# The second transform stage of a fused filter and gated network as three products of high and low parts

## The chip, the core and the metric

The kernel runs on one core of a Trainium2 chip. The metric is the device time of one execution in microseconds (us). Five engines work side by side and meet at semaphores: PE (matrix products), ACT (ScalarE), DVE (VectorE), POOL (GpSimd) and SP (SyncE, which here only issues transfers). Each engine takes its own instructions in the order in which the program lists them. SBUF is the memory on the core, PSUM the banks into which PE writes its sums, DRAM the large memory outside.

## The reference, cut to what matters

```python
X = np.fft.rfft(x, axis=1)                     # x: 8 batches x 3136 x 256
x = np.fft.irfft(X * (filt_r + 1j * filt_i), n=3136, axis=1)
h = np.maximum(x @ w_in, 0.0)                  # 256 -> 1024
conv = sum(conv_w[k] * shifted(h, k - 1) for k in range(3))
out = (h * sigmoid(conv)) @ w_out              # 1024 -> 256
```

Eight batches pass through a filter in the frequency domain, and then through a network whose gate is a convolution of three taps along the sequence.

## The kernel before, in words

**The transform.** A batch has 3136 = 112 x 28 rows of 256 numbers. The transform and its way back are four stages of matrix products, each with 14 operations (`NP`), one for every pair `q` of the 28. The first stage, kind "1", multiplies two blocks of x by tables (`by_column`, L243 to L245, four products in the trace for two in the program). Its sums go from PSUM to SBUF by an ACT copy (`store`, L238 to L241) and from there to DRAM (`a_dram`). The second stage, kind "2", reads them back in another order of rows (`load_in`, L233) and multiplies all 512 columns by one table (`second`, L254, through `by_row`, L247 to L252). `filt` (L260 to L268) multiplies these sums by the filter with three DVE instructions that read the PSUM bank, and POOL adds two parts to `z`. The third stage, kind "3", multiplies `z` by another table (L249 too, operand `z`), and its sums go through `store` to `b_dram`. The fourth, kind "4", reads them back (L275) and leaves the network's input `y`. All four stages are products of fp32 operands.

**The network.** `inner` (L187 to L189) makes one bank of 512 columns of h for one of 8 blocks of 128 features: six products of fp32r operands, that is `mm3` (high by high, high by low, low by high) for two blocks of 128 inputs. `project` makes 12 fp32r products of 256 columns (L536 to L538).

**The order.** The first batch's transform runs alone, in front of the main loop, and ends with two operations "1" of the second batch (`AHEAD`, L402 to L405). The main loop has one iteration, here called a slot, for each block of 510 rows and 128 features, 400 in all, and everything in it stands in program order (`manual_schedule`). A list, `plan`, names for each slot the transform operations of the next batch: 48 slots belong to each batch. Slots are numbered from 0 within the 48 of a batch; batch 1 is the first whose transform lies in the loop, batch 7 the last. For slot m the program lists, in this order:

1. `from_bank` for the transform operations of slot m-1: the ACT copy for kinds "1" and "3", the three DVE instructions for kind "2", a DVE copy for kind "4";
2. `want_in`, which asks for loads ahead;
3. on PE the transform operations of slot m, and then `inner` of slot m;
4. on ACT `relu` and the middle tap `centre` of the network's slot m-1 (L495, L500), then `sigmoid` of slot m-2 (L507); on DVE the first tap of slot m-1 (L504); on ACT the rounding of slot m-3 (L156);
5. on DVE the `gate` of slot m-2 (L510); on POOL the low part of g for slot m-4 (L162); then the steps in a list `later`;
6. on DVE the third tap of slot m-1 (L504), and on PE `project` of slot m-6.

The transform operations share two PSUM banks (pool `ps_t`, `bufs=2`), which they take in turn as they are free. An operation that takes a bank waits until the last reader of the operation that held it before is through. Because PE goes by its list, the `inner` behind such an operation waits too.

Of the kernel before, what the change touches and what calls it, by code (L numbers as in the profile page):

```python
# [132 lines left out]
def tile_fft_filter_gated_ffn(  # L133
# [58 lines left out]
    a_dram = [dram.tile([N2, 112, D], F32, name=f"a_dram{b}") for b in range(B)]  # L192
    b_dram = [dram.tile([N2, 112, D], F32, name=f"b_dram{b}") for b in range(B)]
    a_out = [t[:].rearrange("n p d -> p n d") for t in a_dram]
    a_in = [t[:].rearrange("n (r g) d -> (n r) g d", g=G) for t in a_dram]
# [6 lines left out]
    s2_sb = wc.tile([112, 120], F32, name="s2_sb")  # L202
    s2s_sb = wc.tile([112, 120], F32, name="s2s_sb")
    s3_sb = wc.tile([120, 112], F32, name="s3_sb")
    s3s_sb = wc.tile([120, 112], F32, name="s3s_sb")
    one_sb = wc.tile([128, 128], F32, name="one_sb")
# [26 lines left out]
    def load_in(pool, kind, b, q, bufs, tag):  # L233
        r = pool.tile([112, 2, D], F32, name=tag, bufs=bufs)
        nc.sync.dma_start(out=r, in_={"1": xv, "2": a_in, "4": b_in}[kind][b][:, pair(q)])
        return r

    def store(pool, kind, b, q, ps, bufs, tag, queue=nc.sync):  # L238
        st = pool.tile([112, 2, D], F32, name=tag, bufs=bufs)
        nc.scalar.activation(st, ps[0:112].rearrange("p (j d) -> p j d", d=D), AF.Copy)  # L240
        queue.dma_start(out={"1": a_out, "3": b_out}[kind][b][:, pair(q)], in_=st)  # L241
# [12 lines left out]
    def second(ps, q, r):  # L254
        by_row(ps[0:120], q, r, s2_sb, s2s_sb)

# [28 lines left out]
    def load_weights(k, pool):  # L285
        raws[k] = raw = pool.tile([128, 2, 1024], I32, name="raw", bufs=1 if pool is tp else 2)
        for part, w in enumerate((w_in, w_out)):
            nc.sync.dma_start(out=raw[:, part], in_=w[:, 1024 * k:1024 * k + 1024])
# [7 lines left out]
    def convert(k, pool, n=2):  # L296

        for j in range(2):
            em = pool.tile([128, 2, 2, 256], I32, name="em", bufs=n)
            w = pool.tile([128, 2, 256], F32, name="ws", bufs=n)  # L300
            yield from to_f32(w, raws[k][:, :, 512 * j:512 * j + 512], em[:, 0], em[:, 1])
# [10 lines left out]
    with (  # L312
# [4 lines left out]
        fts, tabs, rows, zs, pss = {}, {}, {}, {}, {}  # L317
        by_r = [sc.tile([120, 4, N2], F32, name=f"by_r{i}", bufs=1) for i in range(2)]
# [32 lines left out]
        with tc.tile_pool(name="sq", bufs=2) as sq:  # L351
# [15 lines left out]
            def first_loads(c):  # L367
                table("1", c)
                r = sq.tile([128, 4, D], F32, name="rows", bufs=5)
# [12 lines left out]
            for q in range(NP):  # L382
                if q % 2 == 0 and q // 2 + 3 < 7:
                    first_loads(q // 2 + 3)
                if q == 8:
                    for k in range(4):
                        load_filter(k)
                    load_weights(2, sc)
                ps = turned_stage(rows["x", q // 2][:, 2 * (q % 2):2 * (q % 2) + 2], [tab("1", q)[:, j] for j in range(2)])
                nc.scalar.activation(at[:, :, pair(q)], ps, AF.Copy)  # L390
                if q >= 1:
                    steps(early, 3 if q < 12 else 2 * (q == 12))
            for t, s in zip(by_r, (s3_sb, s3s_sb)):
                nc.gpsimd.tensor_copy(t, s.rearrange("p (c r) -> p r c", r=4))
            for i in range(NP + 4):
# [18 lines left out]
                if i == 5:  # L414
                    table("1", 0)
                    for q in range(AHEAD):
                        r = sq.tile([128, 2, D], F32, name="xa", bufs=2)
# [189 lines left out]
    stored = {("1", 1): AHEAD}  # L607
# [5 lines left out]
    def want_in():  # L613
        while wanted["in"] < min(done["in"] + 5, len(inputs)) and ready(inputs[wanted["in"]]):
            op = inputs[wanted["in"]]
            wanted["in"] += 1
            got_in[op] = load_in(tp, *op, 5, "tin")
# [13 lines left out]
    def transform(op):  # L631
# [20 lines left out]
    def from_bank(op):  # L652
# [12 lines left out]
    def to_y(op):  # L665
        kind, b, q = op
        if kind == "4":
# [6 lines left out]
    with tc.manual_schedule(engines=COMPUTE | {mybir.EngineType.SP}):  # L674
# [4 lines left out]
        late = convert(3, wp, 1)  # L679
# [80 lines left out]
```

## Time and profile before

| what | before |
|---|---|
| median of 3 runs | 1554.33 us (1551.63 to 1555.62) |
| profiled execution | 1554.59 us |
| its span, first to last instruction | 1552.8 us |
| DVE busy | 1185.3 us, 76% |
| ACT busy | 1144.7 us, 74% |
| POOL busy | 828.3 us, 53% |
| mean clock of PE as granted | 0.997 |
| moved by DMA | 229.49 MB, mean 148 GB/s |

The profile is one execution with the start and length of each instruction. Its duration is not that by which a stream of products advances: products overlap in PE's pipeline, so the step from one start to the next is what a product costs there. A bracket at the end of a timeline row says how long the engine had been idle before the instruction and what released it. The profiled execution's own time is 1.8 us above its span.

### The profile page before, as it was taken

To read this page: it belongs to the slowest core of one execution; us is meant where nothing else is said; L and a number is where in the kernel's file an instruction comes from. 1 tells how busy PE (TensorE), PEld (TensorE's weight loads), DVE (VectorE), ACT (ScalarE), POOL (GpSimd) and SP (SyncE) were. 2 spreads that over 40 slices of the span, in tenths; PEclk is the share of its full clock that TensorE was granted. 3 is DMA by queue.
4 is the path that set the end of the run, shared out by engine and by line. 5 is a ranking of instruction groups with operands and counts; after the bars stand their busy time and mean duration, and the time that the engine had idled before them with its cause. 6 is when DMAs were issued, how large, how long until landed. Compare 5 with 4: busy or idle time off the path is not lost.

```text
span 1552.8 us, 26446 instructions
## 1 busy us (share of the span) xinstructions
PE 1519.7 (98%) x9202; PEld 1290.6 (83%) x9202; DVE 1185.3 (76%) x1810; ACT 1144.7 (74%) x1973; POOL 828.3 (53%) x721
## 2 busy tenths in 40 slices
PE   6999999999999999999999999999999999999999
PEld 5777788877997789877898778987799878999998
DVE  7978766788677877778777776778867888777776
ACT  3576668766896668866787667976688667888886
POOL 4644447545574555645565445744557445664444
PEclk9999999999999999999999999999999999999999
DMA  8867653665436555465544665356543543300000
GB/s 302 256 185 215 208 170 109 181 200 166 135 110 202 179 155 159 121 193 169 177 124 143 185 196 153 97 179 203 165 135 100 160 140 110 101 28 15 28 28 30
DMA packets 158436, 229.49 MB, mean 148 GB/s; under 512 B 16432, under 2 KB 109088, under 8 KB 158304
## 3 DMA queue, kind: packets, MB, share of 16 engines
q1 hardware_dynamic: 157824, 227.35, 48.4%
q8 instruction: 73, 1.20, 0.3%
q14 instruction: 59, 0.48, 0.1%
q10 hardware_dynamic: 480, 0.46, 0.1%
HBM read 157.10 MB, written 70.65 MB: 147 GB/s over the span
## 4 chain that ended last, share of the span: by engine, by line
PE 92%; DVE 2%; ACT 2%; DMA 2%; issue 2%; SPq 0%; POOL 0%; ACTq 0%; POOLq 0%; DVEq 0%
PE ps_h L187 12%; PE ps_h L189 12%; PE ps_h L188 12%; PE po L536 12%; PE po L538 12%; PE po L537 11%; PE ps_t L249 10%; PE ps_t L275 6%; PE ps_t L245 5%; DMA rows<-in_x 1%; PE ps_t L252 1%; ACT br L346 0%; DVE v L265 0%; DVE z L264 0%; DMA f<-in_filt 0%
## 5 line engine op out<-in xcount | busy, mean ns | idle before, releaser
L504 DVE SCALAR_TENSOR_TENSOR t<-ps_h,cw,t 128x510 f32<-128x510 f32 (+1 forms) x800 | 589.1, 737 | 301.5 <-ACT t L500 298.4
L162 POOL TENSOR_TENSOR g<-t,g 128x510 fp32r<-128x510 f32 (+1 forms) x400 | 505.3, 1273 | 203.6 <-ACT g L156 191.9
L536 PE MATMUL po<-wo,g 128*128 128x256 f32 (+1 forms) x1576 | 440.4, 279 | 0.1
L538 PE MATMUL po<-wo,g 128*128 128x256 f32 (+1 forms) x1576 | 439.5, 279 | 0.0
L537 PE MATMUL po<-wo,g 128*128 128x256 f32 (+1 forms) x1576 | 439.3, 279 | 0.0
L495 ACT ACTIVATE ps_h<-ps_h 128x512 f32<-128x512 f32 (+1 forms) x400 | 234.7, 587 | 243.9 <-PE ps_h L189 242.2
L500 ACT ACTIVATE t<-ps_h,cw 128x510 f32<-128x510 f32 (+1 forms) x400 | 272.4, 681 | 102.8 <-POOL g L162 70.1
L267 POOL TENSOR_TENSOR z<-z,v 120x512 f32<-120x512 f32 x112 | 144.8, 1293 | 380.4 <-DVE v L266 312.7
L187 PE MATMUL ps_h<-y,wi 128*128 128x512 f32 (+1 forms) x688 | 333.4, 485 | 0.5 <-DVE y L159 0.5
L536 PEld LDWEIGHTS po<-wo,g 128*128 128x128 f32 (+1 forms) x1576 | 297.0, 188 | 17.3 <-ACT g L156 0.3
L537 PEld LDWEIGHTS po<-wo,g 128*128 128x128 f32 (+1 forms) x1576 | 296.4, 188 | 17.0
L538 PEld LDWEIGHTS po<-wo,g 128*128 128x128 f32 (+1 forms) x1576 | 296.6, 188 | 0.6 <-POOL g L162 0.5
L189 PE MATMUL ps_h<-y,wi 128*128 128x512 f32 (+1 forms) x688 | 270.1, 393 | 0.0
L188 PE MATMUL ps_h<-y,wi 128*128 128x512 f32 (+1 forms) x688 | 270.1, 393 | 0.0
L510 DVE TENSOR_TENSOR t<-ps_h,t 128x510 f32<-128x510 f32 (+1 forms) x400 | 268.6, 671 | 0.9 <-ACT t L507 0.8
L507 ACT ACTIVATE t<-t 128x510 f32<-128x510 f32 (+1 forms) x400 | 245.3, 613 | 1.7 <-DVE t L504 1.6
L156 ACT ACTIVATE g<-t 128x510 fp32r<-128x510 f32 (+1 forms) x400 | 245.1, 613 | 0.2 <-DVE t L510 0.2
L162 POOL TENSOR_TENSOR y<-z,y 128x448 fp32r<-128x448 f32 x98 | 138.5, 1422 | 93.8 <-ACT y L156 91.9
L187 PEld LDWEIGHTS ps_h<-y,wi 128*128 128x128 f32 x688 | 130.4, 189 | 44.3 <-issue 23.6
L188 PEld LDWEIGHTS ps_h<-y,wi 128*128 128x128 f32 x688 | 130.7, 190 | 41.3 <-issue 24.3
L189 PEld LDWEIGHTS ps_h<-y,wi 128*128 128x128 f32 x688 | 130.0, 189 | 30.2 <-POOL wi L162 0.3
L240 ACT ACTIVATE st<-ps_t 112x512 f32<-112x512 f32 x194 | 114.0, 590 | 11.2 <-PE ps_t L245 11.1
(91 smaller groups left out, 1608.0 us busy)
## 6 DMA issues: line engine op xcount, KB each, us to landing
filt<-in_filt SPq DMA_DIRECT2D x98, 512.0 KB
tin<-a_dram SPq DMA_DIRECT2D x98, 224.0 KB
b_dram<-st SPq DMA_DIRECT2D x98, 224.0 KB
tin<-b_dram SPq DMA_DIRECT2D x98, 224.0 KB
tin<-in_x SPq DMA_DIRECT2D x96, 224.0 KB
a_dram<-st SPq DMA_DIRECT2D x96, 224.0 KB
out<-ot SPq DMA_DIRECT2D x45, 256.0 KB
tab<-in_m SPq DMA_DIRECT2D x98, 98.0 KB
```

The source lines that it names most:

```text
L156: nc.scalar.activation(dst, src, AF.Copy)
L162: nc.gpsimd.tensor_tensor(out=dst, in0=src, in1=hi.bitcast(F32), op=ALU.subtract)
L187: nc.tensor.matmul(ps, lhsT=wh, rhs=rh, start=start, stop=False, **kw)
L188: nc.tensor.matmul(ps, lhsT=wh, rhs=rl, start=False, stop=False, **kw)
L189: nc.tensor.matmul(ps, lhsT=wl, rhs=rh, start=False, stop=stop, **kw)
L500: nc.scalar.activation(t, hs[u, f][:, 1:n + 1], AF.Copy, scale=cw[:, 1, f:f + 1])
L504: nc.vector.scalar_tensor_tensor(out=t, in0=h[:, k:place(u)[2] + k], scalar=cw[:, k, f:f + 1], in1=t, op0=ALU.mult, op1=ALU.add)
L507: nc.scalar.activation(ts[u, f], ts[u, f], AF.Sigmoid)
L510: nc.vector.tensor_mul(ts[u, f], hs.pop((u, f))[:, 1:place(u)[2] + 1], ts[u, f])
L536: nc.tensor.matmul(o, lhsT=gh[:, c:c + n], rhs=wo[0][:, f], start=first, stop=False, skip_group_check=True)
L537: nc.tensor.matmul(o, lhsT=gh[:, c:c + n], rhs=wo[1][:, f], start=False, stop=False, skip_group_check=True)
L538: nc.tensor.matmul(o, lhsT=gl[:, c:c + n], rhs=wo[0][:, f], start=False, stop=last, skip_group_check=True)
```

## The change

The second stage of the seven batches in the loop becomes `mm3`: three fp32r products of 512 columns in place of one fp32 product. Its table is cut once, by four POOL instructions at the end of the first batch's first stage, into a high part and what is left. The sums of the first stage are cut as they leave their bank: ACT writes the high part where the copy stood, and a new DVE instruction subtracts it from the sum, read from the bank once more, and writes the low part. Both go to DRAM (`a_dram`, and the new `r_dram`), and both are loaded, 224 KB each, for the second stage. The DVE instruction and its transfer stand in `later`, behind the gate and ahead of the third tap; only then is the operation counted as stored. To make room, loads for kind "2" get a pool of their own (`tia`, 3 buffers), `tin` has 3 buffers in place of 5, the tiles for stores become two of `st` and two of `sh`, `rows` has 4 in place of 5, and the early conversion of weights borrows `tia` and `st`. The first batch's second stage stays one fp32 product.

```diff
-        st = pool.tile([112, 2, D], F32, name=tag, bufs=bufs)
...
+    def split_store(pool, b, q, ps, queue=nc.sync):
+        st = pool.tile([112, 2, 2, D], F32R, name="sh", bufs=2)
+        p = ps[0:112].rearrange("p (j d) -> p j d", d=D)
+        hi_act(st[:, 0], p)
+        queue.dma_start(out=a_out[b][:, pair(q)], in_=st[:, 0].bitcast(F32))
+
+        def rest():
+            lo_dve(st[:, 1], p, st[:, 0])
+            queue.dma_start(out=r_out[b][:, pair(q)], in_=st[:, 1].bitcast(F32))
+        return rest
...
+    def load_in(pool, kind, b, q):
+        if kind == "2":
+            r = pool.tile([112, 2, 2, D], F32R, name="tia", bufs=3)
+            for h, t in enumerate((a_in, r_in)):
+                nc.sync.dma_start(out=r[:, h].bitcast(F32), in_=t[b][:, pair(q)])
+            return r
+        r = pool.tile([128, 2, D], F32, name="tin", bufs=3)[0:112]
...
+    def second_split(ps, q, r):
+        if q < NP - 1:
+            mm3(ps[0:120], *second_parts[0], *(r[:, h].rearrange("p j d -> p (j d)") for h in range(2)))
+        else:
+            for j, parts in enumerate(second_parts):
+                mm3(ps[0:120, j * D:j * D + D], *parts, r[:, 0, j], r[:, 1, j])
...
+            for (h, l), t in zip(second_parts, (s2_sb, s2s_sb)):
+                nc.gpsimd.tensor_copy(h, t)
+                lo_pool(l, t, h)
...
-                    store(tp, "1", 1, i - NP, ps, 3, "st", nc.scalar)
+                    split_store(tp, 1, i - NP, ps, nc.scalar)()
...
-        while wanted["in"] < min(done["in"] + 5, len(inputs)) and ready(inputs[wanted["in"]]):
+        while wanted["in"] < min(done["in"] + 6, len(inputs)) and ready(inputs[wanted["in"]]):
             op = inputs[wanted["in"]]
+            if sum((o[0] == "2") == (op[0] == "2") for o in got_in) == 3:
+                break
...
-            second(ps, q, r)
+            second_split(ps, q, r)
...
-        if kind in "13":
-            store(tp, kind, b, q, ps, 3, "st")
+        if kind == "1":
+            rests[op] = split_store(tp, b, q, ps)
+        if kind == "3":
+            store_third(tp, b, q, ps)
...
+        if kind == "1":
+            def rest():
+                rests.pop(op)()
+                stored[kind, b] = stored.get((kind, b), 0) + 1
+            return rest
```

Line numbers in the rows below are those of the kernel before where the row is of before, and of the changed kernel otherwise: there L187 to L189 are the three products of `mm3`, L261 is `by_column`, L265 a product of the third stage, L256 the store of the third stage, L156 a high part on ACT, L159 a low part on DVE, L544 a tap, L550 the gate, L288 to L290 the filter, L535, L540 and L547 `relu`, `centre` and `sigmoid`.

On PE, batch 3, slot 23, before: an operation of the third stage and one of the second, each with what it waits for. The two wait for a bank through ACT's and DVE's semaphore:

```order
L249 MATMUL ps_t_5847<-z_5749,s3_sb_78 112x512 [waits Activation_49,Pool_49]
L249 MATMUL ps_t_5849<-tin_5610,s2_sb_76 120x512 [waits DMAHW7_49,DVE_49]
```

The same place of the changed kernel:

```order
L265 MATMUL ps_t_6089<-z_5986,s3_sb_88 112x512 [waits DVE_49,Pool_49]
L187 MATMUL ps_t_6091<-tia_5916,s20_84 120x512 [waits DMAHW4_49,Activation_49]
L188 MATMUL ps_t_6091<-tia_5916,s20_84 120x512 [waits DMAHW5_49]
L189 MATMUL ps_t_6091<-tia_5916,s21_85 120x512
```

The two banks have changed places. The operation of the second stage takes the bank of the third-stage operation just ahead of it, and so waits for the ACT instruction that stores `ps_t_6089`. That instruction, the last of these rows of ACT, stands behind the network's work of one slot:

```order
L156 ACTIVATE sh_6084<-ps_t_6049 112x512 [waits DMAHW6_49,DMAHW0_49,PE_49]
L535 ACTIVATE ps_h_6054<-ps_h_6054 128x512 [waits PE_49]
L540 ACTIVATE t_6105<-ps_h_6054,cw_90 128x510 [waits Activation_49,Pool_49]
L547 ACTIVATE t_6062<-t_6062 128x510 [waits DVE_49]
L156 ACTIVATE g00_924<-t_6014 128x510 [waits PE_49]
L256 ACTIVATE st_6127<-ps_t_6089 112x512 [waits DMAHW6_49,PE_49]
```

On DVE, the start of batch 1 in the changed kernel, slot 2: `sh_1017` and `sh_1020` are the tiles for slot 1's two operations of the first stage, `t_1045` belongs to the network's slot 1, `t_1006` to its slot 0:

```order
L544 SCALAR_TENSOR_TENSOR t_1045<-ps_h_998,cw_90,t_1045 128x510 [waits Activation_49]
L550 TENSOR_TENSOR t_1006<-ps_h_966,t_1006 128x510 [waits Activation_49]
L159 TENSOR_TENSOR sh_1017<-ps_t_988,sh_1017 112x512 [waits DMAHW3_49,DMAHW1_49,PE_49]
L159 TENSOR_TENSOR sh_1020<-ps_t_993,sh_1020 112x512 [waits DMAHW4_49,DMAHW2_49,PE_49]
L544 SCALAR_TENSOR_TENSOR t_1045<-ps_h_998,cw_90,t_1045 128x510 [waits DVE_49]
```

The two L159 are new; the banks `ps_t_988` and `ps_t_993` are read by them last, where ACT's copy was the last reader before.

More of the change, by code (lines that the diff above doesn't have):

```diff
@@ L192, in tile_fft_filter_gated_ffn @@
     a_dram = [dram.tile([N2, 112, D], F32, name=f"a_dram{b}") for b in range(B)]
+    r_dram = [dram.tile([N2, 112, D], F32, name=f"r_dram{b}") for b in range(B)]
     b_dram = [dram.tile([N2, 112, D], F32, name=f"b_dram{b}") for b in range(B)]
-    a_out = [t[:].rearrange("n p d -> p n d") for t in a_dram]
-    a_in = [t[:].rearrange("n (r g) d -> (n r) g d", g=G) for t in a_dram]
+    a_out, r_out = ([t[:].rearrange("n p d -> p n d") for t in ts] for ts in (a_dram, r_dram))
+    a_in, r_in = ([t[:].rearrange("n (r g) d -> (n r) g d", g=G) for t in ts] for ts in (a_dram, r_dram))
     b_out = [t[:].rearrange("n (r g) d -> (n r) g d", g=G) for t in b_dram]
@@ L201, in tile_fft_filter_gated_ffn @@
     wc = ctx.enter_context(tc.tile_pool(name="wc", bufs=1))
-    s2_sb = wc.tile([112, 120], F32, name="s2_sb")
-    s2s_sb = wc.tile([112, 120], F32, name="s2s_sb")
+    second_parts = [[wc.tile([112, 120], F32R, name=f"{n}{h}") for h in range(2)] for n in ("s2", "s2s")]
     s3_sb = wc.tile([120, 112], F32, name="s3_sb")
     s3s_sb = wc.tile([120, 112], F32, name="s3s_sb")
-    one_sb = wc.tile([128, 128], F32, name="one_sb")
     cw = wc.tile([128, 3, NF], F32, name="cw")
@@ L231, in pair, with store_third @@
         return slice(2 * q, 2 * q + 2)
-    def load_in(pool, kind, b, q, bufs, tag):
-        r = pool.tile([112, 2, D], F32, name=tag, bufs=bufs)
-        nc.sync.dma_start(out=r, in_={"1": xv, "2": a_in, "4": b_in}[kind][b][:, pair(q)])
-        return r
-    def store(pool, kind, b, q, ps, bufs, tag, queue=nc.sync):
-        st = pool.tile([112, 2, D], F32, name=tag, bufs=bufs)
+    def load_in(pool, kind, b, q):
[5 more added lines that the diff above has]
+        r = pool.tile([128, 2, D], F32, name="tin", bufs=3)[0:112]
+        nc.sync.dma_start(out=r, in_={"1": xv, "4": b_in}[kind][b][:, pair(q)])
+        return r
+    def split_store(pool, b, q, ps, queue=nc.sync):
[7 more added lines that the diff above has]
+        return rest
+    def store_third(pool, b, q, ps):
+        st = pool.tile([128, 2, D], F32, name="st", bufs=2)[0:112]
         nc.scalar.activation(st, ps[0:112].rearrange("p (j d) -> p j d", d=D), AF.Copy)
-        queue.dma_start(out={"1": a_out, "3": b_out}[kind][b][:, pair(q)], in_=st)
+        nc.sync.dma_start(out=b_out[b][:, pair(q)], in_=st)
     def by_column(ps, w, r):
@@ L285, in load_weights @@
     def load_weights(k, pool):
-        raws[k] = raw = pool.tile([128, 2, 1024], I32, name="raw", bufs=1 if pool is tp else 2)
+        if pool is tp:
+            raws[k] = [pool.tile([128, 2, 2, D], F32R, name="tia", bufs=3).rearrange("p a j d -> p a (j d)").bitcast(I32) for _ in range(2)]
+            for j in range(2):
+                for part, w in enumerate((w_in, w_out)):
+                    nc.sync.dma_start(out=raws[k][j][:, part], in_=w[:, 1024 * k + 512 * j:1024 * k + 512 * j + 512])
+            return
+        raws[k] = raw = pool.tile([128, 2, 1024], I32, name="raw", bufs=2)
         for part, w in enumerate((w_in, w_out)):
@@ L294, in convert_conv, with convert @@
         yield from to_f32(cw.rearrange("p (o k) f -> p o (k f)", o=1), conv_raw, e, m)
-    def convert(k, pool, n=2):
+    def convert(k, pool):
         for j in range(2):
-            em = pool.tile([128, 2, 2, 256], I32, name="em", bufs=n)
-            w = pool.tile([128, 2, 256], F32, name="ws", bufs=n)
-            yield from to_f32(w, raws[k][:, :, 512 * j:512 * j + 512], em[:, 0], em[:, 1])
+            if pool is tp:
+                if j == 0:
+                    em = pool.tile([128, 2, 2, D], F32R, name="tia", bufs=3).bitcast(I32)
+                w, raw = pool.tile([128, 2, D], F32, name="st", bufs=2), raws[k][j]
+            else:
+                em = pool.tile([128, 2, 2, 256], I32, name="em", bufs=2)
+                w, raw = pool.tile([128, 2, 256], F32, name="ws", bufs=2), raws[k][:, :, 512 * j:512 * j + 512]
+            yield from to_f32(w, raw, em[:, 0], em[:, 1])
             halves = [(t[0][:, j, 256 * k:256 * k + 256], t[1][:, 2 * k + j]) for t in zip(wi, wo)]
@@ L317, in tile_fft_filter_gated_ffn @@
         fts, tabs, rows, zs, pss = {}, {}, {}, {}, {}
+        s2_sb, s2s_sb = (sc.tile([112, 120], F32, name=n, bufs=1) for n in ("s2_sb", "s2s_sb"))
+        one_sb = sc.tile([128, 128], F32, name="one_sb", bufs=1)
         by_r = [sc.tile([120, 4, N2], F32, name=f"by_r{i}", bufs=1) for i in range(2)]
@@ L368, in first_loads @@
                 table("1", c)
-                r = sq.tile([128, 4, D], F32, name="rows", bufs=5)
+                r = sq.tile([128, 4, D], F32, name="rows", bufs=4)
                 nc.sync.dma_start(out=r, in_=xt[0:128, 4 * c:4 * c + 4])
@@ L416, in tile_fft_filter_gated_ffn @@
                     for q in range(AHEAD):
-                        r = sq.tile([128, 2, D], F32, name="xa", bufs=2)
+                        r = tp.tile([128, 2, D], F32, name="tin", bufs=3)
                         nc.sync.dma_start(out=r, in_=xt[N1:N1 + 128, pair(q)])
@@ L605, in tile_fft_filter_gated_ffn @@
     got_in, got_table, got_filter, got_z, banks, vs = {}, {}, {}, {}, {}, {}
-    stored = {("1", 1): AHEAD}
+    stored, rests = {("1", 1): AHEAD}, {}
     def ready(op):
@@ L613, in want_in @@
     def want_in():
-        while wanted["in"] < min(done["in"] + 5, len(inputs)) and ready(inputs[wanted["in"]]):
+        while wanted["in"] < min(done["in"] + 6, len(inputs)) and ready(inputs[wanted["in"]]):
             op = inputs[wanted["in"]]
+            if sum((o[0] == "2") == (op[0] == "2") for o in got_in) == 3:
+                break
             wanted["in"] += 1
-            got_in[op] = load_in(tp, *op, 5, "tin")
+            got_in[op] = load_in(tp, *op)
     def want_table(n):
@@ L678, in tile_fft_filter_gated_ffn @@
         want_filter(0)
-        late = convert(3, wp, 1)
+        late = convert(3, tp)
         for m in range(NF * NU + PLAG + 1):
```

## The prediction

> **What bounds the kernel now.** I read the page first, then the busy time of a long stretch of the loop, then the timeline of single slots.
>
> ```profile
> span 1552.8 us, 26446 instructions
> PE 1519.7 (98%) x9202; PEld 1290.6 (83%) x9202; DVE 1185.3 (76%) x1810; ACT 1144.7 (74%) x1973; POOL 828.3 (53%) x721
> PE 92%; DVE 2%; ACT 2%; DMA 2%; issue 2%; SPq 0%; POOL 0%; ACTq 0%; POOLq 0%; DVEq 0%
> 500.00:700.00 200.00, 199.01 (x1177) 166.97 (x1176) 151.16 (x231) 148.69 (x254) 107.00 (x90) 1.00 0.55 163
> ```
>
> PE is busy for 98% of the span and holds 92% of the chain that ended last. In the window (stretch, length, busy PE, PE's weight loads, DVE, ACT, POOL, clock, share of DMA, GB/s) PE lacks 1 us in 200, at full clock. So time that PE saves is time saved, and any wait put ahead of PE is lost at full price: DVE's and ACT's 25% of idle time doesn't help if one of their instructions comes late.
>
> **The products.** Next come rows of PE's timeline (start, duration, engine, line); what a product costs is the step between starts.
>
> ```profile
> 502.75 0.40 PE L189 MATMUL ps_h<-y,wi 128*128 128x512 f32 x1
> 503.44 0.39 PE L189 MATMUL ps_h<-y,wi 128*128 128x512 f32 x1
> 505.06 1.02 PE L249 MATMUL ps_t<-z,s_sb 120*112 120x512 f32 x2
> 505.92 1.03 PE L245 MATMUL ps_t<-tin,tab 112*112 112x256 f32 x4
> ```
>
> Three fp32r products of 512 columns, from one L189 to the next, step by 0.69 us, 0.23 each. One fp32 product of 512 columns (two records) steps by 0.86. The new second stage therefore saves 0.86 - 0.69 = 0.17 to 0.18 us in each of 98 operations: **-17.4 us**, 2.5 in each of seven batches. The two last pairs in halves (L252) are taken at the same price.
>
> The Trainium skill, "FP8 and Floating Point Precision", section "TensorE Precision Notes", counts four passes for true FP32. By that rule three products save a quarter of 0.86, as an estimate 0.215 us an operation and 21 us in all; the rows above show 3.8 passes, and the sum keeps them.
>
> **What the parts cost.** ACT's high part stands where the copy stood and has its shape. The low part is new on DVE; no such subtraction from PSUM is in the trace, and its nearest row is L264, with as many columns from PSUM and a second operand.
>
> ```profile
> L240 ACT ACTIVATE st<-ps_t 112x512 f32<-112x512 f32 x194 | 114.0, 590 | 11.2 <-PE ps_t L245 11.1
> L264 DVE TENSOR_TENSOR z<-ps_t,filt 120x512 f32<-120x512 f32 x98 | 66.9, 683 | 1.3 <-DMA filt<-in_filt 1.1
> ```
>
> So a low part is 0.69 us (bounds 0.6, the step of a gate from below, and 0.75, a tap). As work on DVE, 98 x 0.69 = 68 us, it fits into 370 us of idle time, and by itself costs nothing. What counts is that a bank of the first stage is now released by DVE, behind the tap and the gate of the slot, and that which operation gets which of the two banks has shifted. From the counts on which the built program's PE waits, I took the releaser of each bank, before and after. Four kinds of wait are new or longer.
>
> **(a) A bank released by the store of the same slot.** The rows to read are one slot's: the last product of an `inner` and the next transform operation on PE, ACT's four instructions, and DVE's tap.
>
> ```profile
> 499.78 0.40 PE L189 MATMUL ps_h<-y,wi 128*128 128x512 f32 x1
> 501.43 1.02 PE L249 MATMUL ps_t<-tin,s_sb 112*120 112x512 f32 x2
> 500.21 0.58 ACT L495 ACTIVATE ps_h<-ps_h 128x512 f32<-128x512 f32 x1 [0.80 <-PE ps_h L189]
> 500.89 0.69 ACT L500 ACTIVATE t<-ps_h,cw 128x510 f32<-128x510 f32 x1
> 501.47 0.62 ACT L507 ACTIVATE t<-t 128x510 f32<-128x510 f32 x1
> 501.99 0.62 ACT L156 ACTIVATE g<-t 128x510 fp32r<-128x510 f32 x1
> 501.61 0.75 DVE L504 SCALAR_TENSOR_TENSOR t<-ps_h,cw,t 128x510 f32<-128x510 f32 x1 [1.98 <-ACT t L500]
> ```
>
> Let T be the end of a slot's `inner` (499.78 + 0.23 = 500.01). PE's next transform operation starts at T + 1.4, and a second one in that slot could at T + 2.25. ACT starts L495 at T + 0.2 and needs 0.68 + 0.58 + 0.52 + 0.52 for its four, then 0.59 for the store of the first operation: T + 3.1. A second operation that takes that bank waits **0.85** at least. Where L500 has itself waited for POOL, it waits longer:
>
> ```profile
> 483.66 1.02 PE L249 MATMUL ps_t<-tin,s_sb 112*120 112x512 f32 x2
> 484.41 0.59 ACT L240 ACTIVATE st<-ps_t 112x512 f32<-112x512 f32 x1
> 556.98 1.02 PE L249 MATMUL ps_t<-tin,s_sb 112*120 112x512 f32 x2
> 557.95 0.69 ACT L500 ACTIVATE t<-ps_h,cw 128x510 f32<-128x510 f32 x1 [2.46 <-POOL g L162]
> 559.57 0.59 ACT L240 ACTIVATE st<-ps_t 112x512 f32<-112x512 f32 x1
> 145.31 1.02 PE L249 MATMUL ps_t<-tin,s_sb 112*120 112x512 f32 x2
> 148.01 0.58 ACT L240 ACTIVATE st<-ps_t 112x512 f32<-112x512 f32 x1
> ```
>
> In batches 2 to 6 this happens in slots 5, 14 and 23. Slot 5: the store ends at 485.00, the product was ready at 483.66, 1.34; one low part (0.69) ahead of the filter, on whose POOL addition POOL's g waits, makes it 2.03. Slot 14: 0.85. Slot 23: 560.16 - 556.98 = 3.18. In batch 1 it is slots 12, 18, 21, 24 and 27 at 0.85 and slot 15 at 148.59 - 145.31 = 3.28.
>
> **(b) A bank released by the filter, with a low part ahead of it.**
>
> ```profile
> 497.69 1.09 PE L245 MATMUL ps_t<-tin,tab 112*112 112x256 f32 x4 [0.25 <-PE ps_t L249]
> 504.92 0.69 DVE L266 SCALAR_TENSOR_TENSOR v<-ps_t,filt 56x512 f32<-56x512 f32 x1
> ```
>
> In slot 8 of batches 2 to 6 the operation already waits for the filter; 0.69 more, and the 0.18 that the product ahead has gained, make +0.87. In slots 10 and 12 the filter ends at 505.61 and, with the low part, at 506.30; the operation is ready at 505.92 - 0.18: +0.56 each.
>
> **(c) A bank released by the low part.** In slot 33 of batches 2 to 6 (slot 35 of batch 1) the second operation of the fourth stage takes the bank of a first-stage operation of the slot before.
>
> ```profile
> 593.63 1.94 PE L275 MATMUL ps_t<-tab,tin 112*128 112x112 f32 x16
> 593.83 0.75 DVE L504 SCALAR_TENSOR_TENSOR t<-ps_h,cw,t 128x510 f32<-128x510 f32 x1 [1.65 <-ACT t L500]
> 594.50 0.68 DVE L510 TENSOR_TENSOR t<-ps_h,t 128x510 f32<-128x510 f32 x1
> 595.09 0.74 DVE L504 SCALAR_TENSOR_TENSOR t<-ps_h,cw,t 128x510 f32<-128x510 f32 x1
> ```
>
> The low part goes in at 595.09 and ends at 595.78; the operation is ready half way through the first row, at 594.52: +1.26. ACT's copy had come earlier.
>
> Batches 2 to 6 together: 2.03 + 0.85 + 3.18 + 0.87 + 2 x 0.56 + 1.26 = 9.3, and five times that **+46.6 us**. Behind each waiting product stand the slot's `inner`, and behind that all of ACT's and DVE's work for it. Batch 1 behind its start: 5 x 0.85 + 3.28 + 1.26, less two waits of 1.0 and 1.2 us (slots 13 and 16) that go since another operation gets the bank: **+6.6 us**. Batch 7 has no first stage beside it: nothing.
>
> **(d) The start of batch 1**, where each of slots 0 to 5 has two operations of the first stage, the most the two banks can hold.
>
> ```profile
> 86.46 1.89 PE L245 MATMUL ps_t<-tin,tab 112*112 112x256 f32 x8
> 90.33 1.89 PE L245 MATMUL ps_t<-tin,tab 112*112 112x256 f32 x8
> 108.50 1.03 PE L245 MATMUL ps_t<-tin,tab 112*112 112x256 f32 x4
> 91.92 1.53 DVE L504 SCALAR_TENSOR_TENSOR t<-ps_h,cw,t 128x510 f32<-128x510 f32 x2 [2.16 <-ACT t L500]
> ```
>
> Before, each slot's two copies ran on ACT ahead of the slot's work, and slots took 3 to 4 us. Now the next slot's operations wait for two low parts, these for the tap of the same slot, this for its `inner`, and this for the operations: a circle. From one second operation to the next: 0.87 + `inner` 1.38 + 0.2 + L495 0.68 + L500 to tap 0.72 + tap 0.66 + gate 0.60 + two low parts 1.38 + 0.05 = 6.5 us. The first round: the tap (91.92) ends at 92.6, two low parts at 94.0. Four more rounds put the last pair's second operation at 120.0, the first of its low parts 5.8 later, and slot 6's operation at 125.9 instead of 108.50: **+17.4 us**. Bounds: four rounds of 5.9, if the two low parts don't stand in a row (+15), and 7.5 below (+21).
>
> A longer round is possible: the two `sh` tiles must also have been stored.
>
> ```profile
> SPq L235 <- DMA a_dram<-st: 16.4, 8, 2.6
> ```
>
> SP waited at most 2.6 us for such a store. The Trainium skill, "DMA: Bandwidth & Descriptors", section "Anatomy of one DMA", gives 2.0 us and the bytes over 436 GB/s; as an estimate 2.5 us for 224 KB. By it the high part, on ACT ahead of L495, starts 2.9 us behind the last low part, a round is about 1 us longer and the time 5 us; the row allows it and doesn't show it.
>
> **(e) The first batch's last steps.** Two low parts now stand on DVE ahead of the last two filters, on which PE waits (through POOL) as late as here:
>
> ```profile
> 63.69 1.15 PE L336 MATMUL ps<-by_r,z 120*128 120x112 f32 x8 [1.16 <-POOL z L267]
> ```
>
> Two low parts (1.38) and a wait of one for ACT's high part (0.59): **+2.0 us**. The four POOL instructions of the table stand where POOL idles; 0.
>
> **(f) Loads.** The second stage now moves 45 MB more, a fifth, and SP issues some 190 transfers more; the DMA engines were busy for 0.55 of the window above. A load asked three operations ahead has two slots, over 7 us. The last first-stage operation of a batch counts as stored one slot later, but four slots lie between. 0, with rival 3 as the other end. Conversions of weights that borrow other tiles: 0; they fill idle DVE time in early slots, which get longer.
>
> **Sum.** -17.4 + 46.6 + 6.6 + 17.4 + 2.0 = +55.2; span 1608.0, and with the 1.8 us around it (the profiled execution took 1554.6, the median is 1554.3) about **1610 us**, 3.6% slower.
>
> **The rivals.**
>
> 1. *Only the shortest waits.* The excess over 0.85 in slots 5, 15 and 23 comes from POOL's g being late. PE's own waits give POOL time to catch up; if it does, batches 2 to 6 pay 3 x 0.85 + 3.25 = 5.8 each, batch 1's rest 4.2: -17.4 + 29 + 4.2 + 17.4 + 2 = +35, about 1590. For it: POOL is busy for 53% only. Against it: L500's 2.46 us come from the filters just ahead, a new pile each time.
> 2. *The other side: no bank is late.* If the banks are read out by the time PE comes, only the gain is left, and (e): 1552.8 - 17.4 + 2 + 1.8 = 1539. It decides in slot 14 and its like: the store would have to end 0.85 us sooner, at T + 2.25, that is ahead of the rounding and the sigmoid in ACT's order, and the low part ahead of the tap on DVE. The order puts both behind.
> 3. *Loads come late as well.* SP waits for the low part before it sends it on, with loads queued behind. If the first load of each of seven batches is late by one slot of 3.65 us, +26: 1636.
> 4. *Gain and waits cancel*, if the waits come to a quarter of the 72.6 us that I count: no change.
>
> The Trainium skill speaks against the change too: "Perfetto Trace Analysis", section "Optimization Strategy", reads a gap that repeats on the busiest engine as a sign that a buffer or PSUM is short. The repeating 0.25 and 1 us before transform operations agree; the new readers hold the same two banks longer.
>
> **How the numbers follow.** The forecast, with the bounds in (a) to (d) 1600 to 1622, gets 0.57; rival 1 0.22; rival 2 0.06; rival 3, up to 1650, 0.12; rival 4 0.03. A measurement of this kernel can tell about 0.3% from no change. Faster 0.07, same 0.03, slower 0.90. The range takes in the forecast, rival 1 down to 1578 (a start round of 5.0), and rival 3's near side: 1578 to 1640.
>
> **What would show it.** In the trace of after: the three products 0.69 apart; second-stage products with idle time ahead of them, released by ACT's store in slots 5, 14 and 23 (0.85 to 3.2 us); first-stage operations at the start of batch 1 about 6.5 us apart, released by DVE's L159; the operation of slot 6 near 126 and not 108; PE's busy share near 95%. I am wrong if PE's idle time stays near 30 us, if the waits name DMA, or if slots 5 to 23 show no gap.

## The result, and the profile after

The changed kernel takes 1677.47 us (median of 4, 1674.02 to 1682.84) against 1553.96 us before: ratio 1.0799, 95% interval 1.0764 to 1.0834. The forecast was 1610 us, 56 us slower; it is 123 us slower, outside the range. The direction held, and the size was less than half of what came.

The page after: span, busy time, the chain that ended last, and three groups (busy time and mean of one, then idle time just before them and its releasers).

```profile
span 1677.8 us, 27098 instructions
PE 1561.7 (93%) x9307; PEld 1341.8 (80%) x9307; DVE 1244.3 (74%) x1908; ACT 1149.2 (68%) x1973; POOL 829.4 (49%) x725
PE 73%; ACT 8%; issue 7%; DVE 4%; DMA 4%; POOL 3%; SPq 0%; ACTq 0%; POOLq 0%; DVEq 0%
L159 DVE TENSOR_TENSOR sh<-ps_t,sh 112x512 fp32r<-112x512 f32 x96 | 64.9, 681 | 0.0
L187 PE MATMUL ps_t<-tia,s 112*120 112x512 f32 x98 | 46.4, 473 | 48.9 <-ACT st L256 41.7 <-PE ps_t L265 3.8 <-issue 2.8
L156 ACT ACTIVATE sh<-ps_t 112x512 fp32r<-112x512 f32 x96 | 57.3, 597 | 71.6 <-DMA r_dram<-sh 46.5 <-PE ps_t L261 18.3 <-PE ps_h L189 6.5
```

PE holds 73% of the chain where it held 92%. A low part takes 0.68 us, as assumed, and 48.9 us of idle time stand ahead of the second stage's first product, 41.7 of them put down to ACT's store: the wait that the prediction named (a). Two things stand in no term of the forecast's sum. PE is 42 us busier, although its products should have taken less; and ACT's high part waits 46.5 us for the store of a low part (the prediction named such a store and left it out of the sum).

Next are four stretches with the same columns as the window of before, whose clock was 1.00 and 0.997 on the whole. They are the start of batch 1; a stretch of the loop; slot 23 of batch 2 up to its second operation; and what follows in that slot.

```profile
86.00:180.00 94.00, 65.94 (x269) 51.37 (x269) 49.80 (x77) 41.11 (x71) 22.70 (x28) 0.78 0.61 179
500.00:700.00 200.00, 188.91 (x1125) 161.60 (x1124) 149.53 (x230) 140.40 (x239) 101.39 (x85) 0.97 0.60 182
431.40:435.40 4.00, 0.95 (x3) 0.11 (x1) 2.70 (x5) 2.21 (x4) 2.97 (x3) 0.93 0.90 267
435.40:441.60 6.20, 6.16 (x20) 5.26 (x21) 3.71 (x6) 1.79 (x3) 2.32 (x2) 0.50 0.26 81
```

The granted clock falls to 0.50 after PE has idled in slot 23, and stays there for the 6 us of the slot's products. The timeline of that slot: PE's second operation, and on ACT the `centre` that waits for POOL, as the prediction had it, and the store that releases PE:

```profile
435.44 0.78 PE L187 MATMUL ps_t<-tia,s 112*120 112x512 f32 x1 [3.09 <-ACT st L256]
436.02 0.63 PE L188 MATMUL ps_t<-tia,s 112*120 112x512 f32 x1
436.44 0.63 PE L189 MATMUL ps_t<-tia,s 112*120 112x512 f32 x1
436.87 0.63 PE L187 MATMUL ps_h<-y,wi 128*128 128x512 f32 x1
437.30 0.63 PE L188 MATMUL ps_h<-y,wi 128*128 128x512 f32 x1
...
433.18 0.69 ACT L540 ACTIVATE t<-ps_h,cw 128x510 f32<-128x510 f32 x1 [2.45 <-POOL g L162]
434.80 0.59 ACT L256 ACTIVATE st<-ps_t 112x512 f32<-112x512 f32 x1
```

The wait is that of the forecast: 3.09 us of idle time, 3.18 forecast. But from 436.44 on products step by 0.43 us in place of 0.23.

At the start of batch 1 a round between two slots lasts 9.8 us, where 6.5 was forecast:

```profile
106.21 3.75 PE L261 MATMUL ps_t<-tin,tab 112*112 112x256 f32 x8 [4.46 <-DVE sh L159]
116.00 2.48 PE L261 MATMUL ps_t<-tin,tab 112*112 112x256 f32 x5 [4.30 <-DVE sh L159]
...
111.47 1.29 ACT L156 ACTIVATE sh<-ps_t 112x512 fp32r<-112x512 f32 x2 [6.77 <-DMA r_dram<-sh]
...
104.37 4.23 SPq L665 DMA_DIRECT2D tab<-in_s  x2
108.69 0.88 SPq L251 DMA_DIRECT2D r_dram<-sh  x2
...
105.48 1.28 DVE L159 TENSOR_TENSOR sh<-ps_t,sh 112x512 fp32r<-112x512 f32 x2
```

The circle is there: PE is released by DVE's low part each time. Inside it the clock is down (the two operations take 3.2 us, to the `inner` at 109.41, not 1.74), and ACT's next high part waits for its tile. Low parts ready at 106.8 are sent only from 108.69, behind a load of a table that held SP, and the tile is free at 111.47.

So two theories beside the banks: **clock** (PE's idle time brings the clock down, and the slot's other work then costs double) and **tile** (one `sh` tile holds both parts, and so the high part waits for the low part's store). The rival of both is that the waits for the banks are simply longer than worked out.

### The profile page after: what moved, and what is told of

It reads as the page before. It is cut to its first block, busy times and chain, and to the rows that moved or that the text cites. A ratio compares the mean times of both kernels' runs of the same rounds, so it can differ in the third digit from the quotient of the medians.

```text
span 1677.8 us, 27098 instructions
## 1 busy us (share of the span) xinstructions
PE 1561.7 (93%) x9307; PEld 1341.8 (80%) x9307; DVE 1244.3 (74%) x1908; ACT 1149.2 (68%) x1973; POOL 829.4 (49%) x725
## 4 chain that ended last, share of the span: by engine, by line
PE 73%; ACT 8%; issue 7%; DVE 4%; DMA 4%; POOL 3%; SPq 0%; ACTq 0%; POOLq 0%; DVEq 0%
PE ps_h L187 10%; PE ps_h L189 10%; PE ps_h L188 10%; PE po L576 9%; PE po L578 9%; PE po L577 9%; PE ps_t L299 5%; PE ps_t L261 4%; PE ps_t L265 3%; POOL g L162 2%; DMA r_dram<-sh 2%; PE ps_t L187 2%; ACT t L540 2%; ACT g L156 1%; ACT ps_h L535 1%
## 5 line engine op out<-in xcount | busy, mean ns | idle before, releaser
L544 DVE SCALAR_TENSOR_TENSOR t<-ps_h,cw,t 128x510 f32<-128x510 f32 (+1 forms) x800 | 588.2, 736 | 352.7 <-ACT t L540 349.6
L535 ACT ACTIVATE ps_h<-ps_h 128x512 f32<-128x512 f32 (+1 forms) x400 | 234.0, 585 | 302.4 <-PE ps_h L189 301.6
L540 ACT ACTIVATE t<-ps_h,cw 128x510 f32<-128x510 f32 (+1 forms) x400 | 272.7, 682 | 93.9 <-POOL g L162 61.2
L576 PEld LDWEIGHTS po<-wo,g 128*128 128x128 f32 (+1 forms) x1576 | 302.6, 192 | 18.0 <-ACT g L156 0.3
L577 PEld LDWEIGHTS po<-wo,g 128*128 128x128 f32 (+1 forms) x1576 | 301.3, 191 | 17.8
L187 PE MATMUL ps_h<-y,wi 128*128 128x512 f32 (+1 forms) x688 | 312.8, 455 | 0.0
L578 PEld LDWEIGHTS po<-wo,g 128*128 128x128 f32 (+1 forms) x1576 | 300.8, 191 | 0.6 <-POOL g L162 0.5
L189 PE MATMUL ps_h<-y,wi 128*128 128x512 f32 (+1 forms) x688 | 275.8, 401 | 0.0
L550 DVE TENSOR_TENSOR t<-ps_h,t 128x510 f32<-128x510 f32 (+1 forms) x400 | 268.5, 671 | 1.2 <-ACT t L547 0.8
L547 ACT ACTIVATE t<-t 128x510 f32<-128x510 f32 (+1 forms) x400 | 245.4, 613 | 4.0 <-DVE t L544 3.9
L156 ACT ACTIVATE g<-t 128x510 fp32r<-128x510 f32 (+1 forms) x400 | 245.0, 613 | 2.5 <-PE po L577 2.1
L187 PEld LDWEIGHTS ps_h<-y,wi 128*128 128x128 f32 x688 | 134.8, 196 | 31.8 <-issue 7.9
L189 PEld LDWEIGHTS ps_h<-y,wi 128*128 128x128 f32 x688 | 134.0, 195 | 31.4
L188 PEld LDWEIGHTS ps_h<-y,wi 128*128 128x128 f32 x688 | 134.9, 196 | 30.0 <-issue 8.6
L261 PE MATMUL ps_t<-tin,tab 112*112 112x256 f32 x384 | 108.9, 412 | 34.3 <-DVE sh L159 23.7
```

What stands on the lines that cost most here:

```text
L156: nc.scalar.activation(dst, src, AF.Copy)
L187: nc.tensor.matmul(ps, lhsT=wh, rhs=rh, start=start, stop=False, **kw)
L188: nc.tensor.matmul(ps, lhsT=wh, rhs=rl, start=False, stop=False, **kw)
L189: nc.tensor.matmul(ps, lhsT=wl, rhs=rh, start=False, stop=stop, **kw)
L535: nc.scalar.activation(hs[u, f], hs[u, f], AF.Relu)
L540: nc.scalar.activation(t, hs[u, f][:, 1:n + 1], AF.Copy, scale=cw[:, 1, f:f + 1])
```

## The experiments

The kernels without a table row or an interval were executed once. Executions of the kernel before lie between 1551.5 and 1557.3 us and those of the changed kernel between 1674.0 and 1682.8, so a few us between two kernels with long waits show nothing. A slot's length is taken on PE from the end of one `inner` to the end of the next.

### Do the banks make the loss? The kernel without the low part

```diff
-            lo_dve(st[:, 1], p, st[:, 0])
-            queue.dma_start(out=r_out[b][:, pair(q)], in_=st[:, 1].bitcast(F32))
+            pass
...
-            for h, t in enumerate((a_in, r_in)):
-                nc.sync.dma_start(out=r[:, h].bitcast(F32), in_=t[b][:, pair(q)])
+            nc.sync.dma_start(out=r[:, 0].bitcast(F32), in_=a_in[b][:, pair(q)])
```

> The changed kernel without the low part: no DVE subtraction, no second store and no second load; the high part is used for both, so the low part of the first stage's sums is left out. The three products, the tiles and the counting stay. Theory 1 (the new readers of the two banks make all the loss): the releasers are those of before, no new wait, only the products' gain: about 1537 us (1553 - 17.4). Rival (fewer tiles for loads and stores, or the products themselves, cost): above 1554 us, with idle time ahead of loads.

Measured: 1557.16 us, ratio to before 1.0012 (1.0001 to 1.0022). All of the loss is gone, but the 17 us of gain don't show. From PE's timeline, as the step from slot to slot against before: in batches 2 to 6 the slots with an operation of the second stage are 0.1 to 0.2 us shorter, as forecast, but for slot 21. Behind the start this comes to 10.4 us and not 17: slots 8 and 39 give some back, and slots 12 and 13 of batch 7 lose 1.6 us, which the profile puts down to no engine. The start is 12.8 us longer, and there PE waits for loads:

```profile
95.53 1.09 PE L259 MATMUL ps_t<-tin,tab 112*112 112x256 f32 x4 [2.24 <-DMA tin<-in_x]
98.65 1.83 PE L259 MATMUL ps_t<-tin,tab 112*112 112x256 f32 x4
```

So the loss comes with the low part (its instruction, its place or its transfers; which of them, the later runs tell), and the rival was partly right too: this kernel has three tiles for these loads in place of five, and the start alone costs most of the gain. In the changed kernel this hides behind the circle.

### Is it the clock? Products that only keep PE busy

Ahead of the second operation of the slots with long waits, 4 to 11 products write the bank that `inner` overwrites next. They stand in time that PE would have idled.

```diff
+            nc.tensor.matmul(ps, lhsT=wi[0][:, 0, 0:128], rhs=wi[1][:, 0, 0:512], start=True, stop=True)
...
+WARM_AT = {12: (1, 11), 15: (1, 11), 24: (1, 6), 35: (1, 4), **{48 * t + s: (1, n) for t in range(1, 6) for s, n in ((5, 7), (23, 11), (33, 5))}}
```

> The changed kernel with idle-time products added: 4 to 11 products of 512 columns whose result is overwritten, ahead of the second operation in the slots of long waits (12, 15, 24, 35 of batch 1; 5, 23, 33 of batches 2 to 6), 1 to 2.5 us of work where PE idles 1.1 to 3.3 us. Theory 2 (PE's idle time lowers the granted clock, and the slot's work then runs at half speed): the waits end as before, the clock stays at 1.0, slot 23 falls from 10.5 to about 7.5 us, and the whole to about 1640 us. Rival (the slots are long for what they wait for alone): no change, 1677 us, or more by the added work.

Measured: 1652.99 us, 24 us less than the changed kernel, by adding work; 13 us above what was expected. Slot 23 of batch 2 again, the added products (L529) and the operation behind them, and a window over the 6.2 us behind the wait, as above:

```profile
427.36 3.13 PE L529 MATMUL ps_h<-wi,wi 128*128 128x512 f32 x11
431.05 0.50 PE L187 MATMUL ps_t<-tia,s 112*120 112x512 f32 x1 [0.55 <-ACT st L256]
431.38 0.40 PE L188 MATMUL ps_t<-tia,s 112*120 112x512 f32 x1
431.61 0.39 PE L189 MATMUL ps_t<-tia,s 112*120 112x512 f32 x1
```

```profile
431.01:437.21 6.20, 6.17 (x32) 4.96 (x33) 5.11 (x8) 2.86 (x6) 2.99 (x3) 1.00 0.27 86
```

The operation still waits for the same store, and starts 4.15 us behind the slot's first (426.90), as it did before (435.44 - 431.33 = 4.11). But the clock stays at 1.00, and the slot is 3.2 us longer than in the kernel before and not 4.7 to 5.0. The rival falls: it would have had no change.

### Is it the tile? High and low parts in tiles of their own

```diff
-        st = pool.tile([112, 2, 2, D], F32R, name="sh", bufs=2)
+        st = [pool.tile([112, 2, D], F32R, name=f"sh{h}", bufs=2) for h in range(2)]
```

> The changed kernel with one tile for the high part and one for the low, two of each, in place of two tiles that hold both. Theory 3a (at the start of batch 1 the round is set by the store of the low part, for which ACT's high part waits): rounds of slots 1 to 5 fall from 9.8 to about 6.5 us, 16 us in all, 1661. Theory 3b (the half clock sets nearly the same round): 0.9 us a round, 5 us in all, 1672.

Measured: 1655.25 us, below both ends of what was expected, though not for the reason of 3a. The start gains 5 us (the `inner` of slot 6 of batch 1 ends 33.9 us later than before, where it was 39.1), as 3b has it. The rest comes from later slots: slot 33 is 1.4 us longer than before in batches 2 to 6, where it was 1.8 to 5.1, and in two of these five batches slot 23 keeps its clock. In the changed kernel ACT's high part had waited 2.0 to 3.2 us for its tile while PE was at slot 32 of each of them.

Both together, with products also ahead of slots 1 to 6 of batch 1:

```diff
+WARM_AT = {**{m: (0, 12) for m in range(2, 7)}, 1: (0, 8), 12: (1, 11), 15: (1, 11), 24: (1, 6), 35: (1, 4), **{48 * t + s: (1, n) for t in range(1, 6) for s, n in ((5, 7), (23, 11), (33, 5))}}
```

> The changed kernel with one tile for the high part and one for the low, and with idle-time products (overwritten, they add nothing to the result) both in the slots of long waits and ahead of slots 1 to 6 of batch 1 (8 and 12 of them). Theory (half the clock, and the store of the low part, are what the start lost beside the circle of the prediction): rounds of the start 6.5 us instead of 9.8, slot 6 of batch 1 about 17 us later than before and not 39, and the whole at about 1553 + 17 + 58 = 1628 us. Rival (late loads set the start): rounds stay above 8.5 us with DMA as the releaser, above 1640 us.

Measured: 1627.86 us. That the sum came out is luck: slot 6 ends its `inner` 24.9 us later than before and not 17, and the rest costs 48 us and not 58. The theory on the start holds in kind, and late loads fall as its cause. The start now goes by rounds of 6.75 to 7.4 us:

```profile
98.05 1.98 PE L261 MATMUL ps_t<-tin,tab 112*112 112x256 f32 x8 [1.03 <-DVE sh L159]
104.80 1.12 PE L261 MATMUL ps_t<-tin,tab 112*112 112x256 f32 x4 [0.63 <-DVE sh L159]
106.27 1.09 PE L261 MATMUL ps_t<-tin,tab 112*112 112x256 f32 x4 [0.35 <-DVE t L551]
112.11 1.12 PE L261 MATMUL ps_t<-tin,tab 112*112 112x256 f32 x4 [0.60 <-DVE sh L159]
```

This kernel has the waits of the changed one for the banks, without the halved clock (it is at 1.00 through the whole loop) and without the shared tile: its span is 73.3 us above before. Of the changed kernel's 125.1 us the tile accounts for 24.4 (to the run before this one) and the halved clock for another 27.4, each from one execution of a kernel. The two overlap, since a wait that the tile makes longer brings the clock down too.

### What takes the waits away

First, the low part ahead of the tap and the gate, right behind the high part:

```diff
-            rests[op] = split_store(tp, b, q, ps)
+            split_store(tp, b, q, ps)()
+            stored[kind, b] = stored.get((kind, b), 0) + 1
```

> The changed kernel with the low part made at once, right behind the high part, ahead of the tap and the gate on DVE. Theory 1 (the place of the low part closes the circle at the start and moves the banks): the operations of slots 1 to 6 no longer wait for the network's work of the same slot, slots 12, 15, 23 and 33 lose their waits: 1555 to 1580 us. Rival (DVE waits for ACT's high part with the taps queued behind, and gives it back): above 1600 us.

Measured: 1583.91 us, 4 us above what was expected. Behind the start little is left: 0.6 us in slot 14 and 1.0 us in slot 23 of each batch.

```profile
396.90 0.49 PE L187 MATMUL ps_t<-tia,s 112*120 112x512 f32 x1 [0.90 <-DVE sh L159]
```

The second operation of slot 23 no longer waits for the store of the same slot's first: here its releaser is a low part. The start still costs 26.6 us up to slot 6, now with loads as the releaser, here ahead of slot 1's second operation:

```profile
99.06 2.02 PE L261 MATMUL ps_t<-tin,tab 112*112 112x256 f32 x4 [4.03 <-DMA tin<-in_x]
```

Second, the slot's inner products between its two operations:

```diff
-            for op in new:
+            for op in new[:1]:
                 transform(op)
             if a := at(m):
                 inner(*a)
+            for op in new[1:]:
+                transform(op)
```

> The changed kernel with the slot's six inner products listed between its two transform operations, not behind both. Theory (the second operation's wait for a bank is what holds the inner products): 1.38 us of work covers the waits of 0.85 in slots 14, 18, 21, 27, slots 5, 15, 23 keep 0.8 to 1.9 us and the clock stays up there; the start's circle stays: about 1620 us. Rival (the operation comes late for the filter and the store of the next slot instead): above 1660 us.

Measured: 1613.25 us, 7 us below what was expected, although the clock did not stay up. Slot 5 is 0.85 us longer than before in place of 2.2 to 3.7, and slot 23 1.8 to 2.2 in place of 4.7 to 5.0: the 1.38 us of `inner` cover that much of the wait. But the 1.72 to 1.77 us of idle time left in slot 23 still bring the clock down in four of five batches, and slot 24 pays 1.2 to 1.6 us for it. The start is not helped, with rounds near 10 us.

Third, three banks:

```diff
-    ps_h = ctx.enter_context(tc.tile_pool(name="ps_h", bufs=4, space=bass.MemoryType.PSUM, reuse_waits="tile"))
-    ps_t = ctx.enter_context(tc.tile_pool(name="ps_t", bufs=2, space=bass.MemoryType.PSUM, reuse_waits="tile"))
+    ps_h = ctx.enter_context(tc.tile_pool(name="ps_h", bufs=3, space=bass.MemoryType.PSUM, reuse_waits="tile"))
+    ps_t = ctx.enter_context(tc.tile_pool(name="ps_t", bufs=3, space=bass.MemoryType.PSUM, reuse_waits="tile"))
```

> The changed kernel with three PSUM banks for the transform and three for the network's inner products, where it has two and four. Theory 1 (two banks are too few for the new readers): no operation takes the bank of its own slot's first operation, slots 5, 12, 14, 15, 23 and 24 lose their waits, the start's circle closes one low part earlier: about 1595 us. Rival (the inner products wait for the gate of three slots before, with three banks): every slot grows, above 1650 us.

Measured: 1572.16 us, 23 us better than expected. Batches 2 to 6 each become about 2 us shorter than in the kernel before. Slots 6 and 8 lose even the waits that they had before, which is 1.4 us of it, and the slots with an operation of the second stage have 0.1 to 0.2 us of gain each; slot 24 gives 0.7 back. The start costs 26.9 us. The missing fourth bank costs the inner products little: the first product of an `inner` waits for the gate, 5.8 us in the whole kernel, where in the changed kernel it waited for nothing.

Then the start's loads: low part first, tiles apart, and five tiles for `tin` (two for `tia`; the weights' conversion borrows a filter tile).

> The low part at once behind the high part, a tile each, five tiles for the loads of the first and fourth stage as before the change, and two in place of three for those of the second. Theory (what is left at the start of batch 1 in the run with the low part first are late loads): the start falls from 23 to under 8 us more than before, about 1565 us. Rival (two tiles for the second stage make its loads late in every batch): above 1584 us.

Measured: 1569.57 us. The start falls from 26.6 to 13.0 us, not below 8; the low parts, which stand behind steps of the weights' conversion on DVE, are the releaser there. Two tiles for the second stage's loads cost nothing that can be seen: batch by batch the distance to before stays at 14 us.

### Together, and what the banks alone are worth

> The low part at once behind the high part, a tile each, five tiles for the first and fourth stage's loads, and three PSUM banks for the transform (three for the inner products). Theory 1 (banks and place are all that stands against the gain): slots 12, 14, 15 and 23 lose the waits left with two banks (14 us), and the products' 17 us are seen behind the start; the start keeps about 12 us: about 1555 us. Rival (three banks cost the inner products time in later slots): above 1565 us.

> As best3, with the high parts of batch 1 sent by ACT's own queue. Theory (at the start SP waits for a high part with the loads queued behind it, and ACT for the tile): the start falls by 3 to 6 us, about 1550 us. Rival (each issue takes 0.35 us of ACT, and the start's round goes through ACT): no change or slower than best3.

> The kernel before, with three PSUM banks for the transform and three for the inner products, and nothing else. Theory 1 (two banks cost the kernel before its 1 and 0.5 us in slots 6, 8, 13 and 16): 1 to 2 us a batch less, about 1543 us. Rival (the inner products wait for their banks): above 1554 us.

| kernel | median, us | ratio to before (95%) |
|---|---|---|
| low part first, tiles apart, `tin` 5, three banks | 1538.79 | 0.9895 (0.9881 to 0.9910) |
| the same, batch 1's high parts on ACT's queue | 1538.57 | 0.9896 (0.9881 to 0.9910) |
| before, three banks | 1541.51 | 0.9920 (0.9903 to 0.9936) |

The first is 16 us better than I had expected of it, 1% below the kernel before and clear of its noise. In its loop PE has no idle time left:

```profile
500.00:700.00 200.00, 200.00 (x1224) 173.47 (x1223) 165.62 (x255) 151.52 (x260) 111.34 (x92) 1.00 0.69 208
```

ACT's queue brings nothing: the rival there held, or SP was no longer late. Most of the gain comes from the banks and not from the split: the kernel before, with three banks, is within 3 us of it, and the two intervals overlap. That kernel came out near its forecast of 1543, but in part elsewhere: slots 6 and 8 of batches 2 to 6 lose 1.0 and 0.5 us, and slot 12 of batch 7 alone 4.0. Against it, in the two profiles, the products save 2.1 to 2.8 us in each of batches 2 to 6, 1.5 behind the start of batch 1 and nothing in batch 7, 13 us together, and the start gives 12 of them back.

## Why the prediction was wrong, point by point

All numbers are us against before, from PE's timelines, each stretch up to where the next slot begins on PE (slot 6 of batch 1: its first transform operation); the last column is the changed kernel with tiles apart and PE kept busy.

| term | forecast | changed kernel | clock and tile taken out |
|---|---|---|---|
| up to slot 0 of batch 1 | 2.0 | 3.6 | 4.9 |
| slots 0 to 5 of batch 1 | 17.4 | 33.5 | 20.1 |
| rest of batch 1 | 4.1 | 16.6 | 7.3 |
| batches 2 to 6 | 34.3 | 70.5 | 42.4 |
| batch 7 | -2.5 | 0.9 | -1.4 |
| sum | 55.2 | 125.1 | 73.3 |

**The products**: right for an operation, 0.1 to 0.2 us in a slot of batches 2 to 6 in the run without the low part. The sum of 17.4 took it that the gain of all 98 operations shortens the kernel. In that run 10.4 us of it did, and in the best version 13; nothing of it is left in batch 7 of either, and the profile doesn't say why.

**(a) to (c), which slots wait, for whom**: right. Here are batches 2 to 6, the forecast of a slot, the changed kernel, and the run with clock and tile taken out. The measured columns are what a slot grew by. In slots 5, 12, 14 and 23, which have an operation of the second stage, its gain of 0.17 is taken off there, and the wait itself is that much longer.

| slot | forecast | changed | clock and tile out |
|---|---|---|---|
| 5 | 2.03 | 2.2 to 3.7 | 2.2 to 3.3 |
| 8 | 0.87 | 0.7 to 0.8 | 0.7 to 0.8 |
| 10, 12 | 0.56 | 0.4 to 0.6 | 0.4 to 0.65 |
| 14 | 0.85 | 0.8 | 0.8 |
| 23 | 3.18 | 4.7 to 5.0 | 3.2 |
| 33 | 1.26 | 1.8 to 5.1 | 1.4 |

**The step that failed** is the price of a wait: "any wait put ahead of PE is lost at full price", its own length and no more. In slot 23 a wait forecast at 3.18 and measured at 3.1 made the slot 4.7 to 5.0 us longer, since the clock stood at 0.50 for 3.4 to 6.8 us from about its end, in three batches into slot 24 for another 1 us. The forecast had a row at clock 1.00, taken where PE lacks 1 us in 200, and didn't ask what the clock does where PE lacks more. In batches 2 to 6 the forecast is 36 us short, and the run with products in the idle time of three slots takes 24 of them away. Of the 70 us short in all, the halved clock makes up 27 once the tile is out, the tile 24, which the sum had at nothing, and longer waits and small terms the other 18. The split between clock and tile depends on which is taken out first.

**(d)** The circle is right, and a round of 6.5 us was measured at 6.75 to 7.4 once clock and tile are out. The longer round, which the prediction named and left out of its sum, came about: it was priced at 1 us a round, for the store's landing alone. The tile was free 2.8 us after that store was issued (108.69 to 111.47), near the prediction's estimate of 2.5. (The Trainium skill, "DMA: Bandwidth & Descriptors", section "Anatomy of one DMA", fits the figures of that estimate to transfers that GpSimd issues; here SP issues them.) What the price lacked is that the store also stood on SP behind a load of a table (4.23 us at 104.37), so low parts of 106.8 were gone from their tile only at 111.47.

**(a) in batch 1** was too small in slots 12 and 24, 0.85 against 2.4 and 1.9 with clock and tile out. All five slots were priced at the least wait, and L500's own wait was counted in slot 15 only.

**(e)** was too small, 2.0 against 3.6. Three other kernels whose program is the same up to there show 3.9, 5.4 and 7.1, so single executions scatter by more than the miss; its cause stays open.

**(f)** Loads at 0 was wrong by 12.8 us (in the run without the low part). It didn't add to the sum, as the circle is longer than the loads are late, but it is what the start costs once the circle is open. (Rival 3, but in one place.)

**Rivals.** *Only the shortest waits* falls: slot 23 waits 3.1 us in each of batches 2 to 6, with `centre` 2.45 us behind POOL in the row above, so POOL didn't catch up. *No bank is late* and *gain and waits cancel* fall with the rows above. The Trainium skill's sentence on gaps that repeat on the busiest engine ("Perfetto Trace Analysis", section "Optimization Strategy") pointed the right way: a third bank takes 105 us off the changed kernel, and 13 off the kernel before.

## What to carry to other kernels

Here a new reader of a shared buffer cost little by its own duration and nearly all by its place: ask what stands ahead of it on its engine, and which operation takes that buffer next. Where the bound engine idles for some us at a stretch, look at the clock row behind the stretch before pricing the wait at its length. And before a stage is made cheaper, see whether one more buffer does as much: here a third bank alone brought 13 of the best version's 16 us.

## What the runs showed of the hardware that I had not expected

Products that compute nothing made the kernel 24 us faster, since they kept the clock up. And what a wait costs the clock depends on where it lies. In the trace of the changed kernel the clock is 1.00 or 0.50, and in the loop it changes only on a grid of 3.41 us. Here are stretches of this grid: the two that share an idle time of 2.13 us in slot 5 of batch 3 (553.04 to 555.17); the one that holds most of an idle time of the same length in batch 5 (946.51 to 948.64), and the next; and four from the wait in slot 23 of batch 2 on:

```profile
550.87:554.28 3.41, 2.17 (x14) 1.33 (x12) 2.09 (x4) 2.10 (x5) 3.23 (x3) 1.00 0.91 227
554.28:557.70 3.42, 2.53 (x12) 2.11 (x13) 1.95 (x4) 0.97 (x3) 0.00 (x0) 1.00 0.58 202
946.82:950.23 3.41, 1.59 (x7) 1.29 (x8) 2.60 (x4) 1.77 (x4) 0.75 (x1) 1.00 0.61 205
950.23:953.64 3.41, 3.41 (x15) 3.12 (x14) 0.69 (x1) 1.79 (x3) 0.00 (x0) 0.50 0.16 46
431.40:434.81 3.41, 0.95 (x3) 0.11 (x1) 2.11 (x4) 1.63 (x4) 2.97 (x3) 1.00 0.95 273
434.81:438.22 3.41, 2.78 (x7) 2.18 (x8) 2.79 (x5) 0.58 (x2) 0.00 (x0) 0.50 0.57 181
438.22:441.64 3.42, 3.42 (x15) 3.13 (x14) 1.55 (x3) 1.79 (x3) 2.36 (x2) 0.50 0.02 5
441.64:445.05 3.41, 3.41 (x19) 2.64 (x19) 1.43 (x3) 1.87 (x4) 1.45 (x2) 1.00 0.19 57
```

In batch 3 the idle time falls on two stretches, PE works 2.17 and 2.53 us of them, and the clock stays. In batch 5 nearly all of it falls on one, PE works 1.59 us, and the next stretch has half the clock, though PE had been at work again for 1.6 us (products step by 0.23 us up to 950.16, by 0.43 from 950.51). In this trace the clock fell behind each stretch in which PE was busy for 0.52 of the time or less, and behind none with 0.60 or more. It came back behind stretches with 0.95 or more, and not behind those with 0.83 or less. So a wait's length alone doesn't decide: 1.65 us in slot 33 were enough where PE worked 1.76 us of the stretch (475.78 to 479.19), and 0.73 us in slots 18 and 21 of batch 1 were not. The same 3.1 us in slot 23 cost the clock in three batches and not in two when the tiles were made apart.

The Trainium skill, "TensorE: Matmul & The Clock Gate", Part 1, section "What's actually happening", tells of a gate that halves the clock after an idle window of about 3.4 us, with windows that run freely, and gives full speed back after a busy one. The halving, the free windows of 3.41 us and the return behind a busy one (438.22 to 441.64) agree. That the window must be idle does not: PE worked 0.95 and 1.59 us in windows that brought the clock down.
